# An mLSTM cell and a gated cosine MLP on one core: q and k fetched once, GpSimd copies, scores half a period earlier

## The chip, the cores and the metric

The kernel runs on one core of a Trainium2 chip. TensorE (PE) multiplies matrices into PSUM, VectorE (DVE) and ScalarE (ACT) work element by element, GpSimd (POOL) does too but from SBUF alone, and SyncE (SP) issues most transfers between HBM and SBUF. Each engine takes its instructions in the order in which they were written, and waits on semaphores of the others. The metric is the device time of one execution in microseconds; the profile is one further execution taken by the hardware profiler.

## The reference

The first block is an mLSTM cell for 4 batches x 8 heads, 768 steps, head size 40. The second takes the cell's output as 3072 tokens of 320 values.

```python
for t in range(S):
    m_new = np.maximum(f_gate[:, :, t] + m, i_gate[:, :, t])
    f_stab = np.exp(f_gate[:, :, t] + m - m_new)
    i_stab = np.exp(i_gate[:, :, t] - m_new)
    C = f_stab * C + i_stab * einsum('bhd,bhe->bhde', vt, kt)
    n = f_stab * n + i_stab * kt
    h_tilde = einsum('bhde,bhe->bhd', C, qt)
    denom = np.maximum(np.abs(einsum('bhd,bhd->bh', n, qt)), 1.0)
    y[:, :, t] = sigmoid(o_gate[:, :, t]) * h_tilde / denom
h = x @ w_in            # (3072, 320) @ (320, 2048)
out = (h * np.cos(h)) @ w_out   # (3072, 2048) @ (2048, 320)
```

w_in and w_out arrive as float64; the kernel turns their bits into float32 itself.

## The kernel before, in words

Time is cut into six chunks of 128 steps. One chunk of one batch, with its 8 heads, is a *cell*; cell n is chunk n // 4 of batch n % 4, so there are 24. Within a cell the recurrence is a masked product: scores k.q for all pairs of steps (`scores`, into two PSUM tiles ps), a decay matrix E, their product (`weigh`, in place in E), and the product with v plus what the state st of the earlier chunks gives (`values`, into vt). E begins as the running maxima M, broadcast to all partitions by a transfer from a DRAM scratch tensor M_d; `decay_exponents` subtracts a table column on VectorE and masks on GpSimd, and `decay` takes Exp on ScalarE. G, another broadcast from scratch (G_d), scales the transposed q (`scale_q`, on GpSimd) for the state's part. `normalize_turned` divides by the denominator and applies the output gate, which `turn_gate` has transposed; GpSimd writes the result to xT, and `fade` decays the state there. `seam` transposes the last 8 dimensions of each head on TensorE (px) and multiplies weighted keys by values (pu); `seam_out` copies px to xT, `state` adds pu to st.

For chunks 1 to 5 q and k are loaded so that VectorE can transpose them in blocks of 32 (`load_two`, `turn_blocks`). A head has 40 dimensions, so the upper 8 need blocks of their own. Before, each of q and k is fetched twice: once to partitions 64j+32 on and once, shifted by 32 columns, to partitions 64j on or below, so that one transpose call finds dimensions 0 to 31 in one block and 32 to 39 in the other.

The MLP is computed for one chunk of all four batches at a time, a *pass* c. Each `Up` multiplies xT by 256 columns of w_in into two PSUM banks (pup). For each bank ScalarE rounds (`near`, L591), VectorE takes the remainder (`rest`, L594), ScalarE takes a Sin (`sin`, L599) and VectorE forms the gated value g (`gate`, L603). `down` multiplies g by w_out into four banks po (L615); its last call of a pass also copies po out (L618) and issues the output transfers.

All orders are written by hand: the whole program stands in `tc.manual_schedule()`, and each engine runs its instructions as the calls stand. `first_cells` computes cells 0 to 3. Then `both_parts(c, b)` is called for six passes and four b; one call is a *period* and has two halves. It computes Ups 2b and 2b+1 of pass c and cell n = 4(c+1)+b of the next pass. In the first half come, in this order, Up(2b), `scores(n)`, near, rest, `weigh(n)`, `decay_exponents(n+1)`, sin and gate, `decay(n+1)`, a `down`, `turn_gate`, `values(n)`, `normalize_turned(n)`; in the second Up(2b+1), `seam(n)`, near, rest, `seam_out`, `state`, sin, gate, `weigh_k(n+1)`, a `down`, `turn_blocks(n+1)`, `scale_q(n+1)`. In pass 0 the periods also convert the weights by `to_float32` (two steps on ScalarE, three on VectorE, an add on GpSimd): three pieces of w_in per b (`pieces`) and eight of w_out in all (`outs`, `next_out`). The last 8 rows of each head in w_in go through a DRAM scratch tensor w_last (`last_rows`).

PSUM has two banks for the cell's tiles (tag a: ps, vt, px and pu take turns), two for pup and four for po. ScalarE reloads its function table when it goes from Exp to Sin; `sin_next` takes a Sin of one element so that the table is there ahead of time.

Of the kernel before, what the change touches and what calls it, by code (L numbers as in the profile page):

```python
# [11 lines left out]
FP = mybir.dt.float32  # L12
# [17 lines left out]
def kernel(  # L30
# [67 lines left out]
    for e in range(2):  # L98
        nc.gpsimd.tensor_copy(out=pick[:, e], in_=ident.rearrange("q (a g i) -> q g a i", a=HP, g=2)[:, :, :, 0:8])
# [12 lines left out]
    raws = {w: [const.tile([128, WR + 32], FP, name=f"{w}r{i}") for i in range(2)] for w in "qk"}  # L112
    for t in raws["q"] + raws["k"]:
        nc.gpsimd.memset(t[:, WR:WR + 32], 0.0)
# [3 lines left out]
    for t in st:  # L118
        nc.gpsimd.memset(t, 0.0)
    og = const.tile([128, B, 3 * C // 32, 32], FP, name="og")  # L120
    nc.gpsimd.memset(og, 0.0)
# [32 lines left out]
    w_last = dram.tile([H * (D - 32), 2 * DFF], I32, name="w_last")  # L154

    def last_rows(f):
        cols = slice(f * 2 * WP, (f + 1) * 2 * WP)
        src = moe_w_in.bitcast(I32).rearrange("(h d) n -> h d n", d=D)[:, 32:D, cols]
        nc.sync.dma_start(out=w_last[:, cols].rearrange("(h i) n -> h i n", h=H), in_=src)

    def weights_in(f):
        for i in range(NK):
            src = [(slice(32 * a, 32 * a + 32), w_in_bits[D * (HP * i + a):D * (HP * i + a) + 32, ts(f, WP)]) for a in range(HP)]
            yield w_in_sb[:, i, ts(f, WP)], bits_in(WP, src, pb, WP)
        src = w_last.rearrange("r (a e n two) -> r e a n two", e=2, n=128, two=2)

        yield (w_in_l[:, ts(f, 2)].rearrange("p a n -> p (a n)"),
               bits_in(256, [(slice(64 * e, 64 * e + 64), src[:, e, ts(f, 2)]) for e in range(2)], pb, WP))
# [11 lines left out]
    M_d = [dram.tile([BH, n * C], FP, name=f"M_d{n}") for n in (1, R)]  # L180
    G_d = dram.tile([BH, R * C], FP, name="G_d")
# [29 lines left out]
    def gates_first():  # L211
# [5 lines left out]
        nc.gpsimd.dma_start(out=M_d[0], in_=M0)  # L217
# [22 lines left out]
    def gates_maxima():  # L240
        nc.vector.tensor_tensor_scan(out=flat[1], data0=flat[4], data1=flat[2], initial=M0[:, last],
                                     op0=OP.add, op1=OP.max)
        nc.gpsimd.dma_start(out=M_d[1], in_=flat[1])
# [7 lines left out]
    def gates_exp():  # L251
        for e in (eG, eW):
            nc.scalar.activation(out=e, in_=e, func=AF.Exp)
        nc.gpsimd.dma_start(out=G_d, in_=eG.rearrange("r c s -> r (c s)"))
# [27 lines left out]
    def qs(n):  # L282
        if n not in early:
            early[n] = early[n + 1] = p2.tile([128, 2, H, 64], FP, name="qs", tag="G")
            nc.gpsimd.memset(early[n][:, :, :, D:64], 0.0)
# [34 lines left out]
    def load_two(n, which="qkKv"):  # L320
        c, b = divmod(n, B)
        m = n // 2 % 2
        for name, src in (("q", q), ("k", k)):
            if name in which:
                src = src.rearrange("b (p j) (c t a) d -> j c t (b p) (a d)", j=2, a=C // 32, t=32)
                for j in range(2):
                    for low in range(2):
                        x = 0 if low else 32
                        dst = raws[name][m][64 * j + 32 * low:64 * j + 32 * low + 32, x:x + WR]
                        nc.sync.dma_start(out=dst.rearrange("t (p x) -> t p x", x=C // 32 * D),  # L330
                                          in_=src[j, c, :, 4 * b:4 * b + 8])
# [5 lines left out]
    def load_E(n):  # L337
# [4 lines left out]
        if c > 0:  # L342
            src = M_d[1][b * H:(b + 2) * H, ts(c - 1, C)]
            nc.sync.dma_start(out=E.rearrange("q b h t -> q (b h) t"), in_=src.unsqueeze(0).to_broadcast([128, 2 * H, C]))
            Es[n + 1] = E[:, 1]
            G = p2.tile([128, 2 * HP, C], FP, name="G", tag="G")
            src = G_d.rearrange("(b p j) t -> j (b p) t", j=2, p=HP)
            for j in range(2):
                nc.sync.dma_start(out=G[64 * j:64 * j + 64], in_=src[j, 4 * b:4 * b + 8, ts(c - 1, C)].unsqueeze(0).to_broadcast([64, 2 * HP, C]))
            Gs[n], Gs[n + 1] = G[:, 0:HP], G[:, HP:2 * HP]  # L350
        elif n not in SPREAD:
            nc.sync.dma_start(out=E[:, n % 2], in_=M_d[0][ts(b, H)].unsqueeze(0).to_broadcast([128, H, C]))
# [63 lines left out]

    def turn_blocks(n):
        m = n // 2 % 2
        qkT[n] = [p1.tile([128, HP, C], FP, name=f"t{i}", tag=f"t{i}") for i in range(2)]
        for i, w in enumerate("qk"):  # L420
            x = 32 + n % 2 * (WR // 2)
# [207 lines left out]
    def first_cells():  # L629
        nc.vector.memset(nil, 0.0)  # L630
        gates_in()
# [8 lines left out]
        last_rows(0)  # L640
        load_E(0)
        load_E(1)
        warm(12)
# [12 lines left out]
        weigh_k(0)  # L656
        load_E(2)
# [20 lines left out]
        weigh_k(1)  # L678
        values(0)
# [17 lines left out]
        last_rows(1)  # L697
# [30 lines left out]
        turn_blocks(B)  # L728
# [5 lines left out]
        state(3)  # L734
        decay_exponents(B)
        load_two(B + 2)
        load_E(B + 2)
        decay(B)
        weigh_k(B)
        scale_q(B)  # L740
        for f in range(2, NF // 4):
            last_rows(f)
# [13 lines left out]

    def both_parts(c, b):

        n = (c + 1) * B + b
        cell = n < N  # L760
        for i in range(2):
            f2 = 2 * b + i
            up = Up(c, f2)
            if cell and i == 0:
                scores(n)
                if c == 0 and b == 0:

                    warm(8, psum_o())
            if cell and i == 1:
                seam(n)  # L770
                if n % 2 == 1 and n + 3 < N:
                    load_two(n + 3, "Kv")
            for e in range(2):
                up.near(e)
            for e in range(2):
                up.rest(e)
            if i == 0:
                if cell:
                    weigh(n)
                    if n + 1 < N:  # L780
                        decay_exponents(n + 1)
                for e in range(2):
                    up.sin(e)
                    up.gate(e)
                if b == 0 and c + 1 < NC:
                    sigmoid(c + 1)

                if c == 0 and b > 0 and pieces:
                    to_float32(*pieces.pop(0))
                if cell and n + 1 < N and (c > 0 or b > 0):  # L790
                    decay(n + 1)
            else:
                if cell:
                    seam_out(n)
                if pieces:
                    to_float32(*pieces.pop(0))
                if cell:
                    state(n)
                for e in range(2):
                    up.sin(e)  # L800
                    up.gate(e)
                while pieces:
                    to_float32(*pieces.pop(0))
                if cell and n + 1 < N:
                    weigh_k(n + 1)
            if f2 > 0:
                down(c, f2 - 1)
            elif c > 0:
                down(c - 1, NF // 2 - 1)
            if cell and i == 0:  # L810
                turn_gate(n)
                values(n)
                normalize_turned(n)
                fade(n)
                if n % 2 == 1 and n + 3 < N:
                    load_two(n + 3, "qk")
                    load_E(n + 3)
                if b == B - 2 and c + 2 < NC:
                    load_o(c + 2)
                if c == 0 and b == 0:  # L820
                    next_out()
                    decay(n + 1)
                elif pieces:
                    to_float32(*pieces.pop(0))
                sin_next()
            if i == 1:
                if c == 0 and b + 2 < B:
                    pieces.extend(weights_in(b + 2))
                for _ in range(min(2, len(outs))):
                    next_out()  # L830
                if cell and n + 1 < N:
# [40 lines left out]
```

## Time and profile before

| What | Value |
|---|---|
| median of 3 runs | 586.41 us (586.16 to 587.54) |
| the profiled execution | 588.54 us, of which span 586.8 |
| busy: PE, DVE, ACT, POOL | 562.0, 361.6, 257.2, 140.7 us |
| granted TensorE clock, mean | 0.968 |
| chain that ended last: PE, DMA, DVE | 82%, 9%, 3% of the span |
| moved by DMA | 58.76 MB, mean 100 GB/s |
| first Up of pass 0 ends, of pass 1 ends, last pass begins | 48.9, 163.6, about 507 us |

The page has the busy times and the span in 40 slices; the chain follows the work back from the last instruction; the timeline lists instructions in order of time, each with its start, its length and what ended the idle time before it. A "x2" merges instructions that follow each other, and the length is then that of the group.

### The profile page before, as it was taken

Reading aid. Unit: us, or ns where it says so; the run is one execution under the profiler, and the core shown is the slowest. Engines: PE = TensorE matmul, PEld = TensorE weight load, DVE = VectorE, ACT = ScalarE, POOL = GpSimd, SP = SyncE. Lnnn points to the kernel's source line nnn. Section 1 sums busy time; section 2 is a strip of 40 time slices with the busy share of each in tenths; the row PEclk is TensorE's granted clock in tenths of the full one; section 3 lists DMA queues with packets and bytes.
Section 4 is the critical chain, followed back from the end, with each engine's and each line's share of the span. In section 5 each row is a group of like instructions: output and inputs, shape, how many; then the busy total and the mean of one; then the engine's idle time right before and its main releaser. Section 6 shows DMA issues by size and latency. Waiting matters only on the chain.

```text
span 586.8 us, 8874 instructions
## 1 busy us (share of the span) xinstructions
PE 562.0 (96%) x3404; PEld 336.7 (57%) x3404; DVE 361.6 (62%) x677; ACT 257.2 (44%) x411; POOL 140.7 (24%) x170
## 2 busy tenths in 40 slices
PE   8997869888999999999999999999999999999997
PEld 5874435454556556556556556566556566555454
DVE  5665997787666666666666666666666575423131
ACT  4857617184264343373343373343374251233222
POOL 6524354343321221221221221221211110000000
PEclk9858979897999999999999999999999999999999
DMA  9999999974814914914824714914910000010001
GB/s 142 226 232 208 229 245 234 202 167 89 153 47 90 167 32 91 153 46 91 155 44 90 143 55 89 173 26 91 153 45 1 1 2 1 0 45 1 0 1 45
DMA packets 125546, 58.76 MB, mean 100 GB/s; under 512 B 61328, under 2 KB 121824, under 8 KB 125504
## 3 DMA queue, kind: packets, MB, share of 16 engines
q1 hardware_dynamic: 125360, 58.00, 51.2%
q8 instruction: 27, 0.44, 0.4%
q0 software_dynamic: 96, 0.18, 0.1%
q14 instruction: 15, 0.12, 0.1%
q10 hardware_dynamic: 48, 0.02, 0.0%
HBM read 54.07 MB, written 5.16 MB: 101 GB/s over the span
## 4 chain that ended last, share of the span: by engine, by line
PE 82%; DMA 9%; DVE 3%; SPq 3%; POOL 2%; issue 1%; ACT 0%; DVEq 0%; ACTq 0%; POOLq 0%
PE po L615 32%; PE pup L583 26%; PE pup L586 8%; PE ps L450 4%; PE vt L474 3%; DMA bits<-in_moe_w_in_dram 3%; PE vt L477 3%; PE pu L547 2%; DMA vs<-in_v_dram 2%; PE ph L466 1%; DMA G<-G_d 1%; PE px L542 1%; DMA kr<-in_k_dram 1%; SPq L335 1%; DMA o<-in_o_gate_dram 1%; DMA qr<-in_q_dram 1%
## 5 line engine op out<-in xcount | busy, mean ns | idle before, releaser
L615 PE MATMUL po<-w_out_sb,g 128*128 128x320 f32 x768 | 222.6, 444 | 1.8 <-POOL w_out_sb L151 1.8
L615 PEld LDWEIGHTS po<-w_out_sb,g 128*128 128x128 f32 x768 | 145.0, 194 | 66.0 <-issue 10.1
L583 PE MATMUL pup<-xT,w_in_sb 128*128 128x512 f32 x384 | 176.7, 603 | 0.8 <-DVE g L603 0.7
L594 DVE SCALAR_TENSOR_TENSOR n<-pup,n 128x512 f32<-128x512 f32 x96 | 61.7, 684 | 159.4 <-ACT n L591 159.4
L591 ACT ACTIVATE n<-pup 128x512 int32<-128x512 f32 x96 | 51.9, 592 | 238.0 <-PE pup L586 237.9
L583 PEld LDWEIGHTS pup<-xT,w_in_sb 128*128 128x128 f32 x384 | 71.7, 192 | 80.2 <-issue 67.9
L599 ACT ACTIVATE n<-n 128x512 f32<-128x512 f32 x96 | 58.8, 630 | 18.6 <-DVE n L594 16.6
L603 DVE SCALAR_TENSOR_TENSOR g<-pup,n 128x512 f32<-128x512 f32 x96 | 61.6, 683 | 1.7
L381 POOL TENSOR_SCALAR_AFFINE_SELECT E<-E 128x1024 f32<-128x1024 f32 x22 | 24.0, 1091 | 133.7 <-DVE E L380 133.7
L586 PE MATMUL pup<-xT,w_in_l 64*128 64x512 f32 x192 | 54.2, 641 | 0.0
L432 POOL TENSOR_TENSOR qG<-t,G 128x512 f32<-128x512 f32 x20 | 25.4, 1271 | 69.6 <-DVE t L423 64.2
L450 PEld LDWEIGHTS ps<-t,t 40*128 40x128 f32 x384 | 26.6, 200 | 21.5 <-issue 21.2
L450 PE MATMUL ps<-t,t 40*128 40x128 f32 x384 | 28.2, 289 | 10.8 <-DVE t L423 10.8
L474 PE MATMUL vt<-E,vs 128*32 128x128 f32 (+1 forms) x640 | 33.7, 283 | 4.3 <-DMA vs<-in_v_dram 4.3
L496 POOL TENSOR_TENSOR xT<-yt,db 128x256 f32<-128x256 f32 x20 | 14.5, 724 | 96.7 <-DVE db L493 96.7
L389 ACT ACTIVATE E<-E 128x1024 f32<-128x1024 f32 x24 | 25.4, 1058 | 26.7 <-POOL E L381 25.4
L586 PEld LDWEIGHTS pup<-xT,w_in_l 64*128 64x128 f32 x192 | 14.4, 184 | 36.4 <-issue 34.9
L477 PE MATMUL vt<-qG,st 128*32 128x128 f32 (+1 forms) x640 | 33.3, 280 | 0.0
L456 DVE TENSOR_TENSOR E<-ps,E 128x512 f32<-128x512 f32 x48 | 30.7, 679 | 2.6 <-PE ps L450 2.6
L389 ACT ACT_TABLE_LOAD x21 | 26.9, 1283 | 0.4
L380 DVE TENSOR_TENSOR E<-E,tab 128x1024 f32<-128x1024 f32 x22 | 26.7, 1214 | 0.0
L474 PEld LDWEIGHTS vt<-E,vs 128*32 128x32 f32 (+1 forms) x640 | 17.9, 109 | 13.1 <-DVE g L603 6.6
(134 smaller groups left out, 518.2 us busy)
## 6 DMA issues: line engine op xcount, KB each, us to landing
E<-M_d SPq DMA_DIRECT2D x10, 1024.0 KB, 6.0
qr<-in_q_dram SPq DMA_DIRECT2D x40, 160.0 KB, 3.8
kr<-in_k_dram SPq DMA_DIRECT2D x40, 160.0 KB, 4.9
G<-G_d SPq DMA_DIRECT2D x20, 256.0 KB, 6.9
bits<-in_moe_w_out_dram SPq DMA_DIRECT2D x8, 640.0 KB, 6.3
bits<-in_moe_w_in_dram SPq DMA_DIRECT2D x32, 128.0 KB, 4.3
out_dram<-o_sb SPq DMA_DIRECT2D x24, 160.0 KB, 1.8
o<-in_o_gate_dram SPq DMA_DIRECT2D x20, 160.0 KB, 6.0
```

Source lines behind the costliest of these rows:

```text
L389: nc.scalar.activation(out=Es[n], in_=Es[n], func=AF.Exp, scale=-1.0)
L450: nc.tensor.matmul(ps[j][:, p], kT[r, p], qT[r, p], start=True, stop=True)
L456: nc.vector.tensor_tensor(out=w, in0=pss[n][j], in1=w, op=OP.mult)
L474: nc.tensor.matmul(vt[32 * a:32 * a + hi - lo, i], vs(n)[:, h, lo:hi], E[:, h], start=True, stop=False)
L477: nc.tensor.matmul(vt[32 * a:32 * a + hi - lo, i], state[:, h, lo:hi], Gs[n][:, h // 2], start=False, stop=True)
L583: nc.tensor.matmul(pu, w_in_sb[:, i, ts(2 * f2 + e, 128)], x(i), start=(i == 0), stop=False)
L586: nc.tensor.matmul(pu, w_in_l[r, f2], x(NK, r), start=False, stop=True)
L591: nc.scalar.activation(out=self.n[e], in_=self.pu[e], func=AF.Copy, bias=0.25)
L594: nc.vector.scalar_tensor_tensor(out=self.n[e].bitcast(FP), in0=self.pu[e], scalar=0.25, in1=self.n[e], op0=OP.add, op1=OP.subtract)
L599: nc.scalar.activation(out=r, in_=r, func=AF.Sin, scale=TWO_PI_DOWN)
L603: nc.vector.scalar_tensor_tensor(out=g, in0=self.pu[e], scalar=TWO_PI, in1=self.n[e].bitcast(FP), op0=OP.mult, op1=OP.mult)
L615: nc.tensor.matmul(po[c][b], gs[c, f][:, ts(b, C)], w_out_sb[:, f], start=(f == 0), stop=(f == NF - 1))
```

## The change

- **Loads.** `load_two` fetches q and k of a pair of cells once, to partitions 64j to 64j+31; `lows(n)` copies dimensions 32 to 39 to the next 32 partitions on GpSimd, four copies for two cells. The bounce through w_last is gone; the last rows of w_in come in four direct transfers per piece.
- **Scratch.** M_d and G_d are laid out by chunk, so that the broadcast for two cells reads one run; G_d is written by two transfers.
- **Clearing.** Memsets of st and parts of the raw tiles move behind `weigh_k(0)` and `weigh_k(1)` (`clear`), `pick` is filled there (`pick_in`), the memset of qs moves to VectorE; two warm-up matmuls fewer.
- **Order of a period.** `scores(n+1)` and `weigh(n+1)` are in the second half of period n; `values(n)` stands right behind Up(2b); `turn_gate`, `normalize_turned`, `lows(n+1)`, `turn_blocks(n+1)`, `decay_exponents(n+1)` and `decay(n+1)` follow the first half's gates; `seam(n)` closes the period. Period 4 (c = 0, b = 0) has an order of its own. `next_out` is called twice at the end of each second half of pass 0, ahead of `down(c, 2b)`, and no longer in the first half of period 4.

The loads and the scratch:

```diff
                 for j in range(2):
-                    for low in range(2):
-                        x = 0 if low else 32
-                        dst = raws[name][m][64 * j + 32 * low:64 * j + 32 * low + 32, x:x + WR]
-                        nc.sync.dma_start(out=dst.rearrange("t (p x) -> t p x", x=C // 32 * D),
-                                          in_=src[j, c, :, 4 * b:4 * b + 8])
+                    dst = raws[name][m][64 * j:64 * j + 32]
+                    nc.sync.dma_start(out=dst.rearrange("t (p x) -> t p x", x=C // 32 * D), in_=src[j, c, :, 4 * b:4 * b + 8])
...
-            src = M_d[1][b * H:(b + 2) * H, ts(c - 1, C)]
-            nc.sync.dma_start(out=E.rearrange("q b h t -> q (b h) t"), in_=src.unsqueeze(0).to_broadcast([128, 2 * H, C]))
+            src = M_d[1][c - 1, b * H:(b + 2) * H].rearrange("h t -> (h t)")
+            nc.sync.dma_start(out=E.rearrange("q b h t -> q (b h t)"), in_=src.unsqueeze(0).to_broadcast([128, 2 * H * C]))
...
+    def clear(i):
+        for w in "qk":
+            for j in (32, 96):
+                nc.gpsimd.memset(raws[w][i][j:j + 32], 0.0)
+        for t in st[2 * i:2 * i + 2]:
+            nc.gpsimd.memset(t, 0.0)
...
+    def lows(n):
+        for w in "qk":
+            t = raws[w][n // 2 % 2].rearrange("q (x d) -> q x d", d=D)
+            for j in (0, 64):
+                nc.gpsimd.tensor_copy(out=t[j + 32:j + 64, :, 0:D - 32], in_=t[j:j + 32, :, 32:D])
```

The new period, which replaces the old loop over its two halves:

```python
up = Up(c, 2 * b)
if first:
    scores(n)
    warm(8, psum_o())
elif cell:
    values(n)
for e in range(2):
    up.near(e)
if first:
    decay(n)
    sin_next()
for e in range(2):
    up.rest(e)
for e in range(2):
    up.sin(e)
    up.gate(e)
if b == 0 and c + 1 < NC:
    sigmoid(c + 1)
if first:
    weigh(n)
    scale_q(n)
    turn_gate(n)
elif cell:
    ...
    turn_gate(n)
    normalize_turned(n)
    fade(n)
if c == 0:
    join()
if more:
    if n % 2 == 1:
        lows(n + 1)
    turn_blocks(n + 1)
    decay_exponents(n + 1)
    decay(n + 1)
if cell:
    sin_next()
if b > 0:
    down(c, 2 * b - 1)
elif c > 0:
    down(c - 1, NF // 2 - 1)

up = Up(c, 2 * b + 1)
if first:
    values(n)
elif more:
    scores(n + 1)
for e in range(2):
    up.near(e)
for e in range(2):
    up.rest(e)
if c == 0:
    join()
for e in range(2):
    up.sin(e)
    up.gate(e)
if first:
    normalize_turned(n)
    fade(n)
while pieces:
    join()
if more and not first:
    weigh(n + 1)
if more:
    weigh_k(n + 1)
    scale_q(n + 1)
if c == 0 and b + 2 < B:
    pieces.extend(weights_in(b + 2))
for _ in range(min(2, len(outs))):
    next_out()
down(c, 2 * b)
if first:
    scores(n + 1)
    weigh(n + 1)
if cell:
    seam(n)
    seam_out(n)
    state(n)
    if n % 2 == 1 and n + 3 < N:
        load_two(n + 3, "Kv")
```

Here `cell` is n < 24, `more` is n + 1 < 24, `first` is c = 0 and b = 0, and `join` converts one piece of w_in if there is one. The first "..." stands for the loads of q, k, E and G for cell n+3 (odd n) and of the output gate, which are issued there as before.

## The prediction

> **What bounds the kernel now.** I read the page first, then the chain of work that ended last, then the order of time inside one period, then the waits of the first pass.
>
> ```profile
> span 586.8 us, 8874 instructions
> ...
> PE 562.0 (96%) x3404; PEld 336.7 (57%) x3404; DVE 361.6 (62%) x677; ACT 257.2 (44%) x411; POOL 140.7 (24%) x170
> ...
> DMA  9999999974814914914824714914910000010001
> ```
>
> TensorE is busy 96% of the span; the DMA engines are full only in the first eight of 40 slices (117 us) and half idle after. So two stages have different limits. The chain in order of time (start, us, what) shows the second:
>
> ```profile
> 246.84 3.43 PE pup L583 x8
> 250.28 1.06 PE pup L586 x4
> 251.33 0.89 PE ps L450 x16
> 252.23 4.50 PE po L615 x16
> ```
>
> From about 149 us TensorE is followed by TensorE. One period (one b of `both_parts`) lasts 246.84 to 268.78 in this view, 21.94 us, and has no slack to give: an order that is better for other engines gains nothing there, and one that makes TensorE wait loses. The first pass is different. From the end of the first Up (48.91) to the same point of pass 1 (163.57) it takes 114.7 us, where four periods of 21.94 less one missing `down` (4.5) would take 83.3. TensorE's rows there:
>
> ```profile
> 134.48 1.13 PE L586 MATMUL pup<-xT,w_in_l 64*128 64x512 f32 x4
> 138.23 2.08 PE L450 MATMUL ps<-t,t 40*128 40x128 f32 x16 [2.62 <-DVE t L423]
> 140.24 6.78 PE L615 MATMUL po<-w_out_sb,g 128*128 128x320 f32 x16
> ```
>
> Scores wait 2.62 us for the transposes, and then scores and `down` take 8.7 us where 5.5 is normal. The windows of that stretch (PE, PEld, DVE, ACT, POOL, clock, DMA share, GB/s) name the reason, a granted clock of 0.50:
>
> ```profile
> 140.00:142.00 2.00, 2.00 (x8) 1.19 (x6) 1.69 (x3) 1.16 (x1) 0.00 (x0) 0.50 1.19 213
> ```
>
> Four such stalls (4.33, 5.54, 2.62 and 2.62 us) were followed by matmuls that took 1.6, 2.2, 1.8 and 3.2 us too long, mean 2.2; stalls of 1.84 and 1.32 by none. Last, the durations that I add up, from one period in order of time:
>
> ```profile
> 236.77 0.29 DVE L486 TENSOR_SCALAR dt<-vt 128x128 f32<-128x128 f32 x1 [0.92 <-PE vt L477]
> ...
> 239.49 0.72 DVE L497 TENSOR_TENSOR yt<-yt,db 128x128 f32<-128x128 f32 x1
> ...
> 251.36 1.09 ACT L591 ACTIVATE n<-pup 128x512 int32<-128x512 f32 x2 [7.33 <-PE pup L586]
> ...
> 252.72 1.23 ACT L599 ACTIVATE n<-n 128x512 f32<-128x512 f32 x2 [0.27 <-DVE n L594]
> ...
> 254.40 1.21 DVE L380 TENSOR_TENSOR E<-E,tab 128x1024 f32<-128x1024 f32 x1
> ...
> 255.68 1.09 POOL L381 TENSOR_SCALAR_AFFINE_SELECT E<-E 128x1024 f32<-128x1024 f32 x1 [7.98 <-DVE E L380]
> ...
> 258.03 1.06 ACT L389 ACTIVATE E<-E 128x1024 f32<-128x1024 f32 x1
> 258.99 0.73 ACT L618 COPY o_sb<-po 128x320 f32<-128x320 f32 x2
> ```
>
> Here the subtraction L380 runs early, right behind `weigh`, and Exp ends long before the next rounding L591.
>
> **The change: the steady periods (passes 1 to 4).** The new order puts, in the first half, VectorE's gates, `turn_gate`, `normalize_turned`, `turn_blocks(n+1)` and only then `decay_exponents(n+1)`; ScalarE issues Exp and the Sin table of cell n+1 ahead of the second half's `near`. So `near` of the second Up is queued behind a chain that begins at the end of the first Up, which I call T:
> - `near` at T+0.05, second Sin ends 2.59 later, the second gate 0.06 on, 0.61 to the next operation: T+3.3
> - `turn_gate` 0.72 (start to start, 92.32 to 93.04), normalisation 2.72 + 0.64: T+7.4
> - two transposes 1.86 (80.05 to 81.91): T+9.25
> - subtraction 1.21, select 0.07 + 1.09: T+11.6
> - Exp 0.96, Sin table 1.29, its one-element use 0.11: the second `near` starts at N = T+14.0.
>
> TensorE reaches the end of the second Up at T+11.0 (values 1.9, `down` 4.4, Up 4.66) and, with scores 0.9 and `down` 4.4, the seam at T+16.3. The seam's two PSUM buffers are those of the scores of n+1, so it waits for `weigh(n+1)`, which now stands behind the second gates: N+3.26+0.68 = N+3.94. Then px 0.33, its copy 0.27, the state product 0.72, hand-overs 0.2, and the next Up 4.66: the next T is N+10.1. Behind the waiting px in TensorE's queue stand the state product and that Up; behind the waiting Exp in ScalarE's stand `near` and both Sins. An even cell's period is 14.0+10.1 = 24.1, **+2.2**.
>
> An odd cell has `lows(n+1)`, four GpSimd copies, behind xT (0.68) and `fade` (1.2); these start at T+6.7, so the copies start at T+8.6. No row shows a copy of 256 elements on 32 partitions. The nearest below and above:
>
> ```profile
> L496 POOL TENSOR_TENSOR xT<-yt,db 128x256 f32<-128x256 f32 x20 | 14.5, 724 | 96.7 <-DVE db L493 96.7
> ...
> L99 POOL COPY pick<-ident 128x64 f32<-128x64 f32 x2 | 0.4, 236 | 0.0
> ```
>
> Between 0.24 and 0.72 I take 0.5, as it has the size of the one and the single input of the other. The k copies end at T+10.6, the transposes at T+11.6 instead of 9.25, so N = T+16.4 and the period is **+4.55** (+4.0 to +5.4 by the ends).
>
> b = 0: `sigmoid` (1.29 + 0.96 + 0.49) ends at T+5.4 and holds `turn_gate` back by 2.1. The four output copies stand between Exp and `near`; they took 3.28 us (258.99 to 262.27), as the third waits for an output transfer. N = T+19.4, **+7.55**.
>
> One pass: 7.55 + 4.55 + 2.2 + 4.55 = 18.85, three passes 56.5. Pass 4 has no state product and no `fade` and its last cell prepares nothing: 7.3 + 3.1 + 1.9 - 0.8 = 11.5. Pass 5 has no cells and stays.
>
> The waits in front of the seam are 1.7 us (even) and 3.4 (odd); at b = 0 two longer ones. The even one is below what slowed the clock, the others above: 3 x 3 + 2 = 11 times 2.2 = 24. By no loss at all it is 0, by the largest row 35. Sum of passes 1 to 4: 68 + 24 = **+92**.
>
> A rule to weigh here is the Trainium skill, "TensorE: Matmul & The Clock Gate", Part 1: the array falls to half rate after an idle window of about 3.4 us. By it only b = 0 and the first pass would pay, eight times some 1.7 us, an estimate from its window, in place of fifteen times 2.2, and the whole sum would be 19 us lower. The trace differs: waits of 2.62 us were followed by a clock of 0.50, so the rows decide.
>
> **The first pass.** Weights are converted by VectorE, 1.53 us for a w_in piece, 1.26 for the last one, 1.8 for a w_out piece, and GpSimd's add follows (1.57 for w_out). Before, `down(0,2b)` used a piece that was converted earlier; now `next_out` converts w_out(2b) behind gates, joins and `weigh` in the very half that uses it. In periods 5 and 6, ScalarE's part of a join delays the second Sins to N+3.5; gates N+4.2, join 5.4, `weigh` 6.65, w_out 8.45, add N+10.1. Then `down` 4.4 + 2.2 (TensorE stood for over 10 us), seam 1.5, Up 4.66: N+22.85. N is T+18.0 (odd, join and copies) and T+15.55 (even, join): 40.9 and 38.4 us. Period 7 has no joins: 16.4 + 20.6 = 37.0. Period 4: Exp(4) and its tables hold the Sins to 53.4, `sigmoid` ends at 57.3, join, transposes and Exp(5) give N = 66.3; w_out(0) is ready at 79.8, `down` ends at 86.4, scores, seam and Up at 94.1, where it was 76.66. Sum: 94.1 + 40.9 + 38.4 + 37.0 = 210.4 against 163.57, **+47**.
>
> **What it saves.** 40 of 80 transfers of qr and kr (6.4 MB), the bounce through `w_last` (4 writes; 8 reads become 16 direct ones) and 512-byte runs of M and G, read as 8 and 4 KB. All are on SP's queue; fewer entries let later ones go earlier. It is worth something only in the full 117 us, and there the chain above ends later than the data: nothing is waited for, so 0 (at most the 31 us in the rivals). After that the share is 0.53 and the data lies a period ahead, also for the Kv loads, which `both_parts` now issues on SP behind the seam, about half a period later than before, and for E and G, which are issued where they were; without that lead a Kv load costs its 8 us to landing. The second G_d issue costs GpSimd 0.55 us, beside the 0.55 that L254 took.
>
> **First cells.** The qs memset that held TensorE 1.02 us leaves GpSimd; `clear` brings eight memsets of 1280 elements (1.1 us each; og's 1536 took 1.38) ahead of the first select (21.73), which comes some 3 us later and makes values(2) late by about 1.8. Net 0 to +1, taken as 0; ends -1.8 and +5.
>
> Sum: 47 + 92 = +139 on the profiled execution's 588.54 (span 586.8, 1.7 around it), which is 2.1 above the median of 586.41: 586.4 + 139 = **725**.
>
> **Rivals.**
> - *Only the steady chain.* The first pass comes out even, because lighter transfers bring weights early enough to be converted in VectorE's gaps. For: DMA share above 1.0 up to 117 us. Against: the order on VectorE is fixed. 586.4 + 92 = 678.
> - *Transfers were the limit* (the other side). The first pass falls to TensorE's 83.3 us: 586.4 - 31 = 555, and the steady periods keep 21.94. It decides if the chain from T to N is at most about 12 us instead of 14.0 to 19.4. For: the 13.2 us of ACT's waits for w_in bits. Against: every row of the chain above.
> - *The clock stays down.* If it is half for most of a period's second half, 4.5 us more in 15 periods: 770.
>
> **How the numbers follow.** The main case 0.72, with its own range from 586.4 + 47 - 9 + 68 - 3 = 689 (no clock loss, short copies) to 755 (largest loss, 3.2 in 15 places, +15; long copies in nine periods, +8; first cells +5; rounded up). Only the steady chain 0.16, clock down 0.05, transfers 0.05, cancelling 0.02. The range 675 to 755 takes in the main case and most of the first rival. Faster 0.05, same 0.01, slower 0.94; 0.3% (1.8 us) is about what this kernel's measurement can tell.
>
> **What would show it.** In passes 1 to 4: ScalarE's rounding for the second Up (L591 before) starts 3 to 8 us after its Up ended, right behind Exp and the Sin table; px waits for `weigh`; periods of 24, 27 and 30 us; a granted clock below 1.00 there. In pass 0: `down(0,2b)` waits for GpSimd's w_out add 7 us or more. The prediction is wrong if `near` is found to start within 1 us of its Up, or TensorE stays at 100% from 160 to 500 us.

## The result, and the profile after

| | before | after |
|---|---|---|
| median of 4 runs, us | 586.97 (586.16 to 588.25) | 728.01 (726.8 to 728.32) |
| the profiled execution, us | 588.54 | 728.13 |
| its span, us | 586.8 | 726.2 |
| first Up of pass 0 ends, us | 48.9 | 50.0 |
| passes 0 to 4, us | 114.7, 87.8, 87.8, 87.8, 84.8 | 169.9, 109.8, 112.3, 111.5, 97.2 |
| from the first Up of pass 5 to the end, us | 75.2 | 75.4 |

The changed kernel takes 1.240 times as long (95% interval 1.237 to 1.243), 141 us more. A pass is counted here and below from the end of its first Up to the same point of the next pass. Of the 139.4 us that the span grew, pass 0 has 55.3, passes 1 to 4 have 82.8, the first cells 1.1 and the rest 0.2.

The page of the changed kernel: the span, the busy times, TensorE's clock and the DMA engines in 40 slices.

```profile
span 726.2 us, 8894 instructions
...
PE 595.7 (82%) x3402; PEld 351.1 (48%) x3402; DVE 363.8 (50%) x679; ACT 256.2 (35%) x412; POOL 163.4 (22%) x213
...
PEclk9778695776969899999898999999998899999999
DMA  9999541603400334220243131243141100000001
```

TensorE is busy 34 us longer than before with two matmuls fewer, because its granted clock is lower (mean 0.896 instead of 0.968); GpSimd has 23 us more, VectorE and ScalarE have what they had. TensorE, VectorE and ScalarE are each busy for a smaller share of the span: they wait for one another. The DMA engines are full only in the first four slices. TensorE's waits (releaser, us in total, times, longest) are:

```profile
PE po L619 <- POOL w_out_sb L154: 60.5, 4, 18.6
PE px L546 <- DVE E L460: 29.1, 14, 3.0
PE po L619 <- ACT o_sb L622: 15.7, 4, 3.9
PE ps L454 <- DVE t L427: 11.1, 13, 3.1
```

The first row is pass 0 alone, once in each of its periods. The second and third are the steady periods, but for 0.8 us of px in period 4. Of the last, 4.4 of 11.1 us are in pass 0, the longest wait among them. Before, TensorE had no wait from 149 us on. One odd period in order of time (start, length, operation), from the end of one first Up, T = 301.84, to the next at 329.72:

```profile
311.60 1.13 PE L590 MATMUL pup<-xT,w_in_l 64*128 64x512 f32 x4
...
313.02 1.21 DVE L378 TENSOR_TENSOR E<-E,tab 128x1024 f32<-128x1024 f32 x1
...
314.46 1.09 POOL L379 TENSOR_SCALAR_AFFINE_SELECT E<-E 128x1024 f32<-128x1024 f32 x1 [2.43 <-DVE E L378]
315.58 1.06 ACT L387 ACTIVATE E<-E 128x1024 f32<-128x1024 f32 x1 [9.76 <-POOL E L379]
316.64 1.28 ACT L754 ACT_TABLE_LOAD   x1
...
318.05 1.05 ACT L595 ACTIVATE n<-pup 128x512 int32<-128x512 f32 x2
...
321.98 0.59 PE L546 MATMUL px<-yt,pick 128*128 128x128 f32 x2 [2.99 <-DVE E L460]
```

The second Up has ended at 312.73. Its rounding (L595) starts at 318.05, right behind subtraction, select, Exp and the Sin table of the next cell, and px waits 2.99 us for `weigh`. The windows behind that wait (PE, PEld, DVE, ACT, POOL, clock, DMA share, GB/s) show the clock:

```profile
322.00:324.00 2.00, 1.65 (x8) 1.35 (x9) 0.52 (x1) 0.27 (x1) 0.00 (x0) 0.56 0.00 0
324.00:326.00 2.00, 2.00 (x7) 1.22 (x7) 0.70 (x2) 0.00 (x0) 0.00 (x0) 0.59 0.08 12
326.00:328.00 2.00, 2.00 (x6) 0.87 (x5) 0.00 (x0) 0.00 (x0) 0.00 (x0) 1.00 0.87 160
```

The first eight matmuls of the next Up, 3.60 us at full speed, took 4.24 there. In pass 0, two of TensorE's four rows for `down(0,2b)`:

```profile
82.94 6.43 PE L619 MATMUL po<-w_out_sb,g 128*128 128x320 f32 x16 [18.61 <-POOL w_out_sb L154]
...
128.42 7.57 PE L619 MATMUL po<-w_out_sb,g 128*128 128x320 f32 x16 [14.74 <-POOL w_out_sb L154]
```

### The profile page after: what moved, and what is told of

The parts are those of the page before. It is cut to its first block, busy times and chain, and to the rows that moved or that the text cites. A ratio compares the mean times of both kernels' runs of the same rounds, so it can differ in the third digit from the quotient of the medians.

```text
span 726.2 us, 8894 instructions
## 1 busy us (share of the span) xinstructions
PE 595.7 (82%) x3402; PEld 351.1 (48%) x3402; DVE 363.8 (50%) x679; ACT 256.2 (35%) x412; POOL 163.4 (22%) x213
## 4 chain that ended last, share of the span: by engine, by line
issue 22%; PE 20%; DVE 11%; POOL 6%; ACT 5%; DMA 0%; POOLq 0%; ACTq 0%
PE pup L587 9%; PE po L619 7%; PE pup L590 2%; DVE t L427 2%; POOL E L379 2%; DVE g L607 2%; DVE E L378 2%; PE pu L551 1%; DVE n L598 1%; ACT L754 1%; POOL qG L436 1%; ACT n L603 1%; ACT n L595 1%; POOL xT L500 1%; DVE dt L494 1%
## 5 line engine op out<-in xcount | busy, mean ns | idle before, releaser
L619 PE MATMUL po<-w_out_sb,g 128*128 128x320 f32 x768 | 239.2, 468 | 76.2 <-POOL w_out_sb L154 60.5
L619 PEld LDWEIGHTS po<-w_out_sb,g 128*128 128x128 f32 x768 | 152.3, 204 | 153.2 <-POOL w_out_sb L154 61.5
L587 PE MATMUL pup<-xT,w_in_sb 128*128 128x512 f32 x384 | 185.0, 627 | 3.1 <-DVE g L607 3.1
L587 PEld LDWEIGHTS pup<-xT,w_in_sb 128*128 128x128 f32 x384 | 76.4, 205 | 83.7 <-issue 71.0
L595 ACT ACTIVATE n<-pup 128x512 int32<-128x512 f32 x96 | 51.6, 588 | 172.0 <-PE pup L590 172.0
L387 ACT ACTIVATE E<-E 128x1024 f32<-128x1024 f32 x24 | 25.4, 1058 | 166.8 <-POOL E L379 165.6
L454 PE MATMUL ps<-t,t 40*128 40x128 f32 x384 | 29.2, 294 | 11.1 <-DVE t L427 11.1
L454 PEld LDWEIGHTS ps<-t,t 40*128 40x128 f32 x384 | 25.8, 199 | 25.3 <-PE pup L590 17.6
L558 ACT COPY xT<-px 128x128 f32<-128x128 f32 x20 | 5.3, 265 | 87.5 <-PE px L546 87.5
L546 PE MATMUL px<-yt,pick 128*128 128x128 f32 x40 | 9.9, 331 | 29.1 <-DVE E L460 29.1
L570 DVE TENSOR_TENSOR st<-st,pu 40x192 f32<-40x192 f32 x32 | 11.3, 352 | 44.7 <-PE pu L551 44.3
L427 DVE STREAM_TRANSPOSE t<-qr 128x512 f32<-128x512 f32 x20 | 21.9, 1097 | 18.2 <-POOL qr L419 18.2
```

The source lines that it names most:

```text
L427: nc.vector.transpose(out=qkT[n][i].rearrange("q p (t a) -> q p a t", t=32), in_=src[:, :, :, 0:32])
L454: nc.tensor.matmul(ps[j][:, p], kT[r, p], qT[r, p], start=True, stop=True)
L587: nc.tensor.matmul(pu, w_in_sb[:, i, ts(2 * f2 + e, 128)], x(i), start=(i == 0), stop=False)
L595: nc.scalar.activation(out=self.n[e], in_=self.pu[e], func=AF.Copy, bias=0.25)
L619: nc.tensor.matmul(po[c][b], gs[c, f][:, ts(b, C)], w_out_sb[:, f], start=(f == 0), stop=(f == NF - 1))
```

## The experiments

None of them leaves out any of the computation. This table has them all; the passes are read from the profiled execution of each.

| kernel | median, us | first Up ends | passes 0 to 4, us |
|---|---|---|---|
| before | 586.8 to 588.5 | 48.9 | 114.7, 87.8, 87.8, 87.8, 84.8 |
| after | 728.0 | 50.0 | 169.9, 109.8, 112.3, 111.5, 97.2 |
| exponents early | 651.8 | 49.4 | 154.3, 95.5, 95.5, 95.5, 85.1 |
| w_out ahead | 695.1 | 49.9 | 136.4, 112.3, 111.6, 110.3, 97.2 |
| adds first | 719.9 | 50.5 | 163.9, 112.3, 111.6, 110.3, 97.2 |
| three moves | 595.9 | 50.8 | 118.6, 88.3, 88.3, 88.3, 84.3 |
| order alone | 693.3 | 48.3 | 164.2, 105.2, 102.4, 102.5, 94.5 |
| loads alone | 587.7 | 52.4 | 108.9, 88.5, 87.8, 87.8, 84.8 |
| clearing late | 586.4 | 51.5 | 108.3, 88.5, 87.8, 87.8, 84.8 |
| blocks first | 574.1 | 54.6 | 98.2, 87.8, 87.8, 87.8, 84.8 |
| old loads, blocks first | 583.6 | 46.2 | 110.9, 87.8, 87.8, 87.8, 84.8 |
| clearing in gaps | 571.8 | 47.3 | 99.2, 87.8, 87.8, 87.8, 84.8 |

### Is it the chain in front of the second rounding?

The changed kernel, with the next cell's subtraction, select and Exp moved ahead, to where VectorE's gates of the first Up end:

```diff
             up.gate(e)
+        if more and not first:
+            decay_exponents(n + 1)
         if b == 0 and c + 1 < NC:
             sigmoid(c + 1)
+        if more and not first:
+            decay(n + 1)
...
             turn_blocks(n + 1)
+        if first:
             decay_exponents(n + 1)
             decay(n + 1)
```

> The changed kernel with one move: the subtraction and mask of cell n+1 stand right behind the first half's gates, and its Exp behind the sigmoid, instead of behind normalisation and transposes (period 4 keeps its order). Theory A (the order on VectorE and ScalarE holds the second near back): Exp ends about 8 us after the first Up, so near of the second Up starts when that Up ends. Even cells fall from 24.1 to 22.0, odd ones to about 24 (scores still wait for GpSimd's copies), b = 0 to about 23; no clock loss but in odd periods. Passes 1 to 4 give back about 65 of 83 us and pass 0 some 5: about 655 us. Rival B (the GpSimd copies or the new transfers are what is waited for): nothing that these wait for moves, under 10 us, 718 to 728.

Measured: 651.79 us (651.14 to 652.44), 76 us under the changed kernel. Its waits:

```profile
PE po L619 <- POOL w_out_sb L154: 43.6, 4, 18.6
PE ps L454 <- DVE t L427: 22.3, 14, 4.3
...
PE px L546 <- DVE E L460: 0.8, 1, 0.8
```

The wait of px for `weigh` went from 29.1 to 0.8 us, and even periods are back at 21.8 us. Odd ones stay at 25.4, because the scores of n+1 now wait for the transposes, which stand behind GpSimd's copies. Passes 1 to 4 gave back 59 us where 65 were expected, and pass 0 15.7 where 5 were. The chain is confirmed, and the copies appear as a second cause, which the run with three moves tests.

### Is pass 0 the conversion of w_out in the half that uses it?

One more piece is converted in period 4, where ScalarE and VectorE had been left with little, so that each later `down(0,2b)` finds its piece done:

```diff
         if c == 0:
             join()
+        if first:
+            next_out()
```

> The changed kernel with w_out converted one piece ahead: one more conversion in the first half of period 4, so that every later down finds its piece ready. Theory A: the four waits of down for GpSimd's w_out add (60.5 us in all) go; in periods 5 to 7 the seam then waits for weigh, which is some 8 us earlier than the add, and period 4 gains about 7: pass 0 shorter by 25 to 35 us, about 698 us, passes 1 to 4 as they are. Rival B (weights arrive late in pass 0, or VectorE's sum of work binds it): conversions only change places, under 8 us, above 720.

Measured: 695.07 us (694.9 to 695.25); pass 0 is 33.6 us shorter and passes 1 to 4 are as they were. TensorE's wait for GpSimd's w_out add fell from 60.5 to 1.1 us. Part of it came back in front of the seam (px for `weigh` 46.5 us instead of 29.1, the longest 9.4, plus 5.7 of scores for the normalisation): once the weights are there, the chain of the first question is next.

### Why was the add even later than forecast?

VectorE's and GpSimd's rows ahead of one of these adds, in the changed kernel:

```profile
122.83 1.04 POOL L392 TENSOR_TENSOR kw<-ks,tab 128x512 f32<-128x512 f32 x1
123.12 1.10 DVE L149 TENSOR_SCALAR w_out_sb<-w_out_sb 128x640 f32<-128x640 f32 x1
123.83 1.51 POOL L436 TENSOR_TENSOR qG<-t,G 128x512 f32<-128x512 f32 x1
124.26 1.43 DVE L151 TENSOR_SCALAR w_out_sb<-w_out_sb 128x640 int32<-128x640 int32 x1
125.73 0.82 DVE L153 SCALAR_TENSOR_TENSOR w_out_sb<-bits,w_out_sb 128x640 int32<-128x640 int32 x1
...
126.69 1.67 POOL L154 TENSOR_TENSOR w_out_sb<-w_out_sb,bits 128x640 int32<-128x640 int32 x1 [1.35 <-DVE w_out_sb L153]
```

The two TENSOR_SCALARs end 0.35 us after GpSimd's operation of that moment has ended (124.22 after 123.87, 125.69 after 125.34). So GpSimd's two multiplications were moved behind the conversions; VectorE's order is untouched:

```diff
-        if more:
-            weigh_k(n + 1)
-            scale_q(n + 1)
         if c == 0 and b + 2 < B:
             pieces.extend(weights_in(b + 2))
         for _ in range(min(2, len(outs))):
             next_out()
+        if more:
+            weigh_k(n + 1)
+            scale_q(n + 1)
```

> The changed kernel with GpSimd's weighted k and scaled q of cell n+1 behind the two conversions of w_out instead of ahead of them; VectorE's order is untouched. Theory (VectorE's w_out piece took 3.35 us instead of the 1.8 that was added up, because its TENSOR_SCALARs wait until GpSimd's multiplications of that moment have ended): the first piece of each period takes VectorE 1.8 us again, its add lands 1.5 to 2 us earlier in all four periods of pass 0, the waits for w_out fall from 60.5 to 53 to 55 us and the time from 728.0 by 5 to 8, to 720 to 723. Rival (VectorE's operations are slow there for a reason of their own, or ScalarE's conversions set the time of the add): the waits stay at 59 to 61 us and the time at 727 to 729.

Measured: 719.91 us (719.52 to 723.01), 8 us less. The waits for w_out are 55.7 us, pass 0 is 6.1 us shorter, and the same three rows are

```profile
122.70 0.48 DVE L149 TENSOR_SCALAR w_out_sb<-w_out_sb 128x640 f32<-128x640 f32 x1
123.22 0.49 DVE L151 TENSOR_SCALAR w_out_sb<-w_out_sb 128x640 int32<-128x640 int32 x1
123.75 0.83 DVE L153 SCALAR_TENSOR_TENSOR w_out_sb<-bits,w_out_sb 128x640 int32<-128x640 int32 x1
```

1.8 us, as against 3.35. The theory holds, though the waits stayed 0.7 us above its range. (The profiled execution, at 723.01, was the slowest of its four; against that of the changed kernel its span is 5.2 us shorter, which is the 6.1 of pass 0 less 0.9 elsewhere.)

### Transfers and order, each alone

First the order of before with everything else of the change: single loads and the copies, scratch by chunk, direct last rows, and the moved clearing. The runs do not tell these parts from one another. The core of it, against the kernel before:

```diff
-                    for low in range(2):
-                        x = 0 if low else 32
-                        dst = raws[name][m][64 * j + 32 * low:64 * j + 32 * low + 32, x:x + WR]
...
+                    dst = raws[name][m][64 * j:64 * j + 32]
...
+                    if n % 2 == 1:
+                        lows(n + 1)
                     turn_blocks(n + 1)
```

> The order of the kernel before, with all of the change that moves data: q and k fetched once, lows on GpSimd ahead of the block transposes, M and G by chunk, last rows of w_in direct, clearing inside the first cells. Theory A: the order costs everything and the data movement nothing; the lighter transfers may save a little of the first pass (its stall of 4.3 us for vs) and GpSimd's four copies may delay a transposition there: 575 to 592 us. Rival B: the copies or the new transfers cost, above 600. Rival C (transfers were the limit of pass 0): 555 to 570.

Measured: 587.71 us (8 runs, 585.97 to 591.54) against 588.33 of before, ratio 0.998 (0.995 to 1.002): no difference. In the profiled executions two effects cancel. Pass 0 is 5.8 us shorter: a wait of 4.33 us for v of cell 4 is gone. The first cells are 3.5 us longer, and GpSimd's rows there show a cause of it:

```profile
18.17 2.35 POOL L120 MEMSET qr<- 32x1280 f32 x2
...
20.57 2.35 POOL L120 MEMSET kr<- 32x1280 f32 x2
...
25.33 1.10 POOL L379 TENSOR_SCALAR_AFFINE_SELECT E<-E 128x1024 f32<-128x1024 f32 x1
```

Eight memsets of 1.16 us stand ahead of selects; this one was at 21.73 before. They need not be all of the 3.5 us: the changed kernel has the same memsets and its select at 24.59, and its first Up ended at 50.0, not 52.4.

Then the new order with the double loads of before, and so without the copies:

```diff
-                    dst = raws[name][m][64 * j:64 * j + 32]
...
+                    for low in range(2):
+                        x = 0 if low else 32
+                        dst = raws[name][m][64 * j + 32 * low:64 * j + 32 * low + 32, x:x + WR]
...
-            if n % 2 == 1:
-                lows(n + 1)
```

> The changed kernel's order with the loads of before: q and k fetched twice, no lows. Theory A: odd periods become like even ones, 24.1 to 24.5 instead of 28 to 29, seven of them, -25 to -32 in passes 1 to 4, and some 5 in pass 0: 690 to 700 us, so the order alone keeps at least 100 of the 141 us. Rival B (the copies are the main cost): under 640.

Measured: 693.34 us (692.41 to 694.27). The order alone costs 105 us, and the loads cost 35 more in this order, where they cost nothing in the old one. Odd periods in passes 1 to 3 are 24.2 to 24.6 us, close to even ones, with one of 25.8 (mean 24.6), where they were 28.5 on average. The copies themselves hold the rounding up by only 2.0 us (16.2 instead of 14.2 behind T); the rest is the clock. Without them px waits 1.7 to 2.2 us in odd periods, and in five of the six the next Up runs at full speed. The period of 25.8 us is the one in which it does not; it stands first here, with one of the five behind it:

```profile
261.20 0.49 PE L548 MATMUL px<-yt,pick 128*128 128x128 f32 x2 [1.73 <-DVE E L462]
...
262.61 5.32 PE L589 MATMUL pup<-xT,w_in_sb 128*128 128x512 f32 x8
...
365.65 0.49 PE L548 MATMUL px<-yt,pick 128*128 128x128 f32 x2 [1.83 <-DVE E L462]
...
367.06 3.62 PE L589 MATMUL pup<-xT,w_in_sb 128*128 128x512 f32 x8
```

The granted clock is 0.50 from 264 to 266 us and 1.00 from 366 to 372.

### Are these all the causes?

The changed kernel with the first two edits, and the copies at the start of the period:

```diff
+        if more and n % 2 == 1:
+            lows(n + 1)
         up = Up(c, 2 * b)
...
         if more:
-            if n % 2 == 1:
-                lows(n + 1)
             turn_blocks(n + 1)
```

> The changed kernel with three moves: the subtraction, select and Exp of cell n+1 behind the first gates, GpSimd's four copies for cell n+1 at the start of the period, and one more w_out piece converted in the first half of period 4. Theory (the rounding of the second Up is queued behind a chain on VectorE, GpSimd and ScalarE, and in pass 0 down(0,2b) waits for a piece converted in the same half): the three costs go nearly altogether. Passes 1 to 3 fall from 110 to 112 us to 88 to 90, pass 4 from 97 to about 85, pass 0 from 170 to 115 to 120; in all 590 to 605 us, where the moves one by one gave 652 and 695. Rival (the second half, with the seam as its close, scores ahead and PSUM's two buffers shared by both, has no slack of its own): the odd periods stay at 24 us or more even with the copies early, passes 1 to 3 at 93 or more, in all 615 to 640 us.

Measured: 595.92 us (595.64 to 596.21), 1.013 times before (1.009 to 1.017). Of 141 us, 132 are gone by three moves that leave the loads and the early scores in place: the early exponents alone were worth 76, the w_out piece alone 33, and the copies are given the remaining 23. That fits: in passes 1 to 4, which the w_out piece left as they were, this kernel is 22.6 us under the one with early exponents, and odd periods are 21.8 us instead of 25.4. In the steady passes only the first period is longer than before, 22.8 us instead of 21.9, so the early scores cost next to nothing there, and gain nothing either. Pass 0 is still 3.9 us longer than before: period 4, which has an order of its own, takes 44.6 us instead of 27.8, and the three behind it 74.0 instead of 86.9.

### From the loads to a faster kernel

The kernel with the loads alone had two things to mend. First its raw-tile clearing, as one block behind `weigh_k(3)`:

```diff
     def clear(i):
-        for w in "qk":
-            for j in (32, 96):
-                nc.gpsimd.memset(raws[w][i][j:j + 32], 0.0)
...
         weigh_k(3)
+        clear_raws()
```

> The order of before with the single loads, in which GpSimd clears the raw tiles behind the last weigh_k of the first cells instead of ahead of their selects. Theory (the 3.5 us that the first cells lost with the single loads are GpSimd's clearing ahead of a select that VectorE waits for): the first Up ends at about 49 us instead of 52.4, and the time is 582 to 586 us, under before's by 0.3 to 1%. Rival (the loss is in the transfers, for instance the later landing of q, k or the weights): the first Up stays at 52 us and the time at 587 to 589.

Measured: 586.43 us (10 runs), ratio 0.997 (0.994 to 1.000), and the first Up at 51.5 us: neither expectation. The selects were early again, but the block now stood ahead of the next things in GpSimd's queue:

```profile
36.08 2.35 POOL L125 MEMSET kr<- 32x1280 f32 x2
38.52 1.28 POOL L157 TENSOR_TENSOR w_in_sb<-w_in_sb,bits 128x512 int32<-128x512 int32 x1
...
39.86 0.84 POOL L422 COPY qr<-qr 32x256 f32<-32x256 f32 x2
40.73 1.10 DVE L430 STREAM_TRANSPOSE t<-qr 128x512 f32<-128x512 f32 x1 [4.79 <-POOL qr L422]
```

VectorE's transposes waited 4.79 us for the copies, its conversion of w_in was behind them, and the first Up waited 6.1 us for w_in. Then, in the same kernel, copies, transposes and scaled q of cell n+1 ahead of the w_out conversions in pass 0:

```diff
-                for _ in range(min(2, len(outs))):
-                    next_out()
                 if cell and n + 1 < N:
...
                     scale_q(n + 1)
+                for _ in range(min(2, len(outs))):
+                    next_out()
```

> The same with VectorE's transposes, GpSimd's copies and scaled q for cell n+1 ahead of the conversion of w_out at the end of each second half of pass 0. Theory (what is left of pass 0's loss is that scores wait for the transposes, 12.2 us over four periods, and that TensorE's clock halves behind these waits): pass 0 falls from 109 to about 98 to 103 us, in all 570 to 580 us, faster than before by 1.5 to 2.5%. Rival (the conversions are the limit there, so that down waits for w_out instead of scores for the transposes): pass 0 stays within 2 us of 109 and the time at 582 to 586.

Measured: 574.13 us (574.02 to 578.11), ratio 0.978 (0.974 to 0.982). Pass 0 is 98.2 us: the scores' wait for the transposes (10.6 us in four periods) is gone, and the waits for w_out have grown from 2.8 to 5.8 us. (The profiled execution took 578.11 us, the other three 574.0 to 574.2, so its first Up at 54.6 us is a late one.) Last, the clearing in the gaps of GpSimd's own queue:

```diff
         pick_in(0)
+        clear_raws(3)
...
         gates_diagonal()
+        clear_raws(1)
         decay(2)
         weigh_k(2)
+        clear_raws(3)
...
-        clear_raws()
...
         scale_q(B)
+        clear_raws(1)
```

> The kernel with blocks first, in which GpSimd's eight memsets of the raw tiles stand in the gaps of its own queue instead of in one block behind the last weigh_k: three while it waits for the running maxima (4.0 us), one between the select and weigh_k of cell 2, three ahead of the select of cell 3 (a wait of 4.6 us), one at the end of the first cells. Theory (behind weigh_k the block of 9.6 us delayed the adds of w_in, so that the first Up waited 5.9 us for them): that wait goes, the first Up ends at 47.5 to 50 us instead of 51.5 to 54.6, and the time is 568 to 572 us. Rival (the adds were late because of VectorE's conversions and the landing of the bits, not because of GpSimd's queue): the wait stays above 4 us and the time at 573 to 576.

Measured: 571.78 us (571.41 to 571.83), ratio 0.972 (0.969 to 0.976), with the first Up at 47.3 us. It beats both kernels, and its page is

```profile
span 569.9 us, 8917 instructions
...
PE 554.0 (97%) x3404; PEld 331.3 (58%) x3404; DVE 365.4 (64%) x679; ACT 256.5 (45%) x411; POOL 165.5 (29%) x213
...
PEclk9969889999999999999999999999999999999999
```

Pass 0, at 99.2 us, is 15.9 above the 83.3 that the prediction estimated for TensorE alone: 6.8 us are waits for w_out, 3.4 the two slow `down` behind them, and what makes the rest stays open.

Is this the loads at all, or could the kernel before have had it by the order? It was run with transposes and scaled q ahead of the w_out conversions, and nothing else:

```diff
-                for _ in range(min(2, len(outs))):
-                    next_out()
                 if cell and n + 1 < N:
                     turn_blocks(n + 1)
                     scale_q(n + 1)
+                for _ in range(min(2, len(outs))):
+                    next_out()
```

> The kernel before, untouched but for VectorE's transposes and GpSimd's scaled q of cell n+1, which go ahead of the conversion of w_out in pass 0; double loads, no copies. Theory (the 14.0 us that the last two kernels gained hold about 10 of this order and about 6 of the lighter transfers): the time is 576 to 580 us, and TensorE still waits some 4 us for v of cell 4, or for other data in pass 0. Rival (all of the gain is the order): 570 to 573 us, as with the single loads. Second rival (the double loads keep q and k so late that the order gains nothing): 584 to 588 us.

Measured: 583.64 us (10 runs, 581.37 to 586.54), ratio 0.995 (0.993 to 0.997), between the theory and the second rival. The scores no longer wait for the transposes, but pass 0 is 110.9 us, and other waits have taken the place:

```profile
PE vt L474 <- DMA vs<-in_v_dram: 7.0, 1, 7.0
PE po L615 <- POOL w_out_sb L151: 5.8, 3, 3.1
PE px L542 <- DVE yt L497: 4.9, 2, 3.3
```

The first row, data that comes late, is absent in the loads alone and in the three kernels built on them, so it is what the lighter transfers remove. The loads alone gave nothing that can be measured, this order alone 0.5%, and the two with the clearing in gaps 2.8%.

## Why the prediction came out as it did

It gave 725 us and 728.0 was measured. The mechanisms were those named, but the closeness is partly luck: two terms were off by 8 to 10 us, in opposite directions.

**The chain from T to N.** Forecast 14.0, 16.4 and 19.4 us for even, odd and first periods; measured 14.2 (403.97 behind 389.81), 16.2 and 19.5. Even periods: forecast 24.1, measured 24.2. The early exponents took this wait away and 76 us with it, so it is shown. The copies took 0.39 us each and not 0.5, and the odd N came 0.2 earlier.

**The clock loss, +24, was too large.** Passes 1 to 4 came out at +82.8 instead of +92. Odd periods were forecast at 28.7 and were 27.9 to 29.5 in passes 1 to 3, mean 28.5; their Ups and state products lost 1.6 us in the one shown above and 3.1 in the next, so 2.2 was a fair mean. The first periods of a pass were forecast at 31.7 and were 29.8, 30.8 and 29.8. There `down` ran slow, 6.3 to 7.9 us instead of 4.57, but beside the chain: in two of the three px still waited 0.2 to 0.4 us for `weigh` when `down` had ended. The prediction added the loss to the path without asking what lay beside it; in the first periods 0.3 to 1.3 of the 2.2 us count, as they would have been 29.5 without any. Pass 4 was 3.5 us too dear.

The rule of the Trainium skill that was weighed ("TensorE: Matmul & The Clock Gate", Part 1, half rate after some 3.4 us idle) would have made the sum 19 us lower. For passes 1 to 4 it would have given some 75, an estimate from its window, about as far below the measured 82.8 as +92 is above, so the size does not decide. The rows decide against its figure: the waits of 2.99 us were followed by a clock of 0.56 in the period shown and 0.50 in the next odd one.

**Pass 0, +47, was too small: +55.3.** By periods, 47.6, 43.9, 41.2 and 37.3 us were measured where 45.2, 40.9, 38.4 and 37.0 were forecast. The waits for w_out (18.6, 14.7, 15.6 and 11.6 us) are there as named. The failing step is "1.8 for a w_out piece": in periods 5 and 6 it was 3.35, which put the add of period 5 at N+12.1 instead of N+10.1. In period 7 it was 1.8, and that period was right. Moving GpSimd's multiplications restored the 1.8 and took 6.1 us off pass 0, out of 8.5 above the forecast by periods; of the 2.4 that are left 1.5 are in period 4, and their cause stays open. The profile of before could have warned: of its eight w_out pieces four took 2.95 to 3.05 us, and 1.8 is the time of the shortest. One of the long ones stands here, with GpSimd's add beside it:

```profile
77.24 1.68 POOL L151 TENSOR_TENSOR w_out_sb<-w_out_sb,bits 128x640 int32<-128x640 int32 x1 [0.81 <-DVE w_out_sb L150]
```

```profile
77.55 1.73 DVE L148 TENSOR_SCALAR w_out_sb<-w_out_sb 128x640 int32<-128x640 int32 x1
```

The loss of clock behind the wait was 3 us in `down` in periods 5 to 7 and not 2.2. N itself was 18.65 instead of 18.0.

**The transfers, 0, and the first cells, 0 to +1.** Right in sum, for the whole and for the first cells (+1.1). With the old order the loads show what they hold: pass 0 gains 5.8 us and the first cells lose 3.5 in the profiled executions. The prediction had named the clearing as a cost there; what the runs show of it is that putting it into gaps made the median 2.4 us shorter than as one late block. That the chain ends later than the data in pass 0 is so in the new order; in the old one v of cell 4 was late.

**The rivals.** "Only the steady chain" fell with pass 0 at +55.3. "Transfers were the limit" fell with the loads alone, which moved the old kernel by nothing, and with the chain at 14 to 19.5 us instead of 12. "The clock stays down" fell: the windows show it back at 1.00 some 4 us behind px, and no odd period reached 30 us.

## What to carry to other kernels

On engines that take their work in order, preparing the next cell is free only where it stands behind what the critical engine needs next; here a subtraction, a select and an Exp with its table ahead of one rounding cost 76 us and four small copies 23, where the lighter transfers alone gained nothing that could be measured. When an order is changed, write down for each engine what its next urgent instruction is queued behind, and put filling work, clearing too, into gaps of that queue that the trace shows. A saving in transfers and a new order are worth trying each alone and together: here the first was worth nothing, a small move in the old order 0.5%, and both with well-placed clearing 2.8%.

## What the hardware showed that was not expected

VectorE's TENSOR_SCALAR on 128x640 took 0.48 us alone and up to 1.74 beside a GpSimd multiplication or add, ending 0.35 to 0.36 us after it in the rows shown; SCALAR_TENSOR_TENSOR on the same piece, 0.82 alone, took 1.54 beside GpSimd's `weigh_k` in period 4. The Trainium skill, "SBUF — State Buffer", section "SBUF: two separate sides", states that the port pair which VectorE shares with GpSimd is an exclusive lock held for a whole instruction. These rows agree with a lock, as VectorE's operation ends only after GpSimd's; why it then needs 0.35 us and not the 0.48 it takes alone, they do not show.

The length of a wait did not decide whether TensorE was slow behind it. With the order alone, a wait of 1.73 us was followed by the slow Up shown there, and one of 2.21 us by an Up at full speed:

```profile
311.67 0.49 PE L548 MATMUL px<-yt,pick 128*128 128x128 f32 x2 [2.21 <-DVE E L462]
...
313.08 3.63 PE L589 MATMUL pup<-xT,w_in_sb 128*128 128x512 f32 x8
```

In the kernel with the clearing in gaps, a wait of 1.79 us was followed by a `down` of 6.26 instead of 4.57:

```profile
76.36 6.26 PE L622 MATMUL po<-w_out_sb,g 128*128 128x320 f32 x16 [1.79 <-POOL w_out_sb L157]
```

The slow stretch can also begin later. In the kernel with late clearing, a wait of 2.99 us was followed by scores at almost full speed and only then by such a `down`; the granted clock was 1.00 up to 82 us, 0.50 from 83 to 85 and 1.00 again from 86:

```profile
81.12 1.16 PE L457 MATMUL ps<-t,t 40*128 40x128 f32 x16 [2.99 <-DVE t L430]
82.22 6.26 PE L622 MATMUL po<-w_out_sb,g 128*128 128x320 f32 x16
```

The Trainium skill, "TensorE: Matmul & The Clock Gate", Part 1, says that its window is free-running. That would let the clock fall sooner or later behind waits of one length, but its idle window of about 3.4 us is longer than each of these waits. No run here tests what decides a single case, and it stays open.

Two kernels with the same first cells (late clearing and blocks first) had their first Up end at 51.5 and 54.6 us in their profiled executions, and so had before and the old loads with blocks first, at 48.9 and 46.2. A difference of a few microseconds there between single profiles, the 3.5 us of the loads alone included, says little.
